# Sliding-window attention with SwiGLU on one core: V kept twice in DRAM in lines of 32-token rows, and projected by residue classes

## The chip, the core and the metric

The kernel runs on one core of a Trainium2 chip. The time is device microseconds of one execution. TensorE (PE) multiplies matrices into PSUM, VectorE (DVE), ScalarE (ACT) and GpSimd (POOL) work on SBUF and PSUM, and SyncE (SP) issues nearly all DMA transfers, which 16 DMA engines carry out. Each engine runs its instructions in order and waits on semaphores.

## What is computed

One transformer block with modulated layer norms, S = 2048 tokens, D = 512, 32 heads of 16, F = 1792. Each query sees W = 8 keys at distances 0, 2, ..., 14 before it.

```python
sa, ca, ga, sb, cb, gb = split(silu(c) @ w_mod, 6)
h = layernorm(x) * (1 + ca) + sa
q, k, v = heads(h @ wqkv)
idx = pos[:, None] - 2 * arange(8)[None, :]        # masked where idx < 0
attn = softmax(where(mask, einsum('hsd,hswd->hsw', q, k[idx]) / 4, -1e9))
x = x + ga * (einsum('hsw,hswd->hsd', attn, v[idx]) @ wo)
h = layernorm(x) * (1 + cb) + sb
x = x + gb * ((silu(h @ w1) * (h @ w3)) @ w2)
```

## The kernel before, in words

The 2048 tokens are 16 tiles T of 128. `LN1` (L270) groups the tiles for the first layer norm and the projections of q, k and v: two, two, four, four, four tiles. `BLOCKS` (L266) groups them for the softmax, `FFN` (L265) for the second layer norm and the FFN. The body of `_build` records operations by `p.op` and `p.dma` in a natural order, numbered from 0. The order in which they are issued on each engine is the list `ORDER` (L980) of these numbers, and the buffer of each tile is in `SLOTS` (L1028). Both lists are the output of a planner that worked with the costs that stand in the calls; for a DMA, `packet_ns` (L70) gives the time of one run, and loads marked `again` count 126 ns a run (L128). `synchronize` (L165) derives the semaphore waits from the operations' reads and writes; transfers of one `group` share one semaphore.

Layer norm writes normalized tiles, which are transposed by TensorE (L636) or by DMA (L617, issued at L124), and modulated by ScalarE (L621, L644) into `vh.at`, a buffer of 128 features by 4 feature blocks by up to 512 tokens. `proj_qk` (L675, matmuls L691) makes q and k with tokens along the free dimension. `proj_v` (L705) makes V of one tile with the tokens on the partitions: the weights of the matmul at L711 are 128 consecutive token columns of `vh.at`, the moving operand is the V part of `wqkv`. ScalarE evicts it (L721) with the heads innermost, and one DMA (L725) writes the tile as 128 rows of 1 KB to the scratch tensor `v_dram` in DRAM, which begins with 16 zero rows (L444).

The logits of a tile come from one multiplication on VectorE (L742, q against eight shifted views of k) and a sum over each head by TensorE (L752). After the softmax the attention weights are transposed by TensorE (L807) and copied to `val` (L811). `values` (L815) then does the weighted sum. Partition (s, w), with s = 0..15 and w = 0..7, gets copies of V's rows: group g = 2q + y of eight holds token 32q + 2s + y − 2w of the tile. Four DMAs, one for each q, load them (L820), each as 128 runs of 2 KB, two neighbouring tokens. So each row of V is read eight times. The load of tile T waits for the stores of T and T − 1, or of T and the zero rows. VectorE multiplies by the weights (L827), TensorE sums over the window (L855), ScalarE evicts (L861), a DMA transposes (L862), TensorE multiplies by `wo` (L867), and VectorE adds to x (L871).

The FFN (L883 up and gate, L889 silu, L892 product, L921 and L909 down) of the first tiles starts while the attention of later tiles still runs. `vshpool` has two buffers, and a third one, `vsh_x`, once the QKV weights are no longer read. Lines that matter for the change: L128, L340, L444, L705 to L726, L802 to L808, L815 to L822, L855 and L943 to L944, and the two lists.

Of the kernel before, what the change touches and what calls it, by code (L numbers as in the profile page):

```python
# [10 lines left out]
P = 128  # L11
S = 2048
D = 512
H = 32
DH = 16
W = 8
DIL = 2
F = 1792
NT = S // P
KT = D // P  # L20
NF = F // P
PAD = 16
EPS = 1e-5
# [50 lines left out]
class Program:  # L74
# [41 lines left out]
    def dma(self, out, in_, key, packets, r=(), w=(), part=(), after=(), eng="sp", cost=450, group=None, transpose=False,  # L116
# [11 lines left out]
        ns = 600 if transpose else each * (126 if again else packet_ns(size))  # L128
# [144 lines left out]
def _build(p, A_x, A_wqkv, A_wo, B_w1, B_w3, B_w2, c, w_mod, out):  # L273
# [66 lines left out]
    v_dram = nc.dram_tensor("v_scratch_dram", (PAD + S, D), bf)  # L340
# [103 lines left out]
    p.dma(v_dram[0:PAD, :], zrow[:], ("load", 11), (16, 1024), r=[vzrow] + wm_hold, w=[vvpad], store=True)  # L444
# [260 lines left out]
    def proj_v(T, tt, vh):  # L705
# [3 lines left out]
        def mm(e, ts):  # L709
            for t in ts:  # L710
                ins = e.matmul(bank(vp), vh.at[:, t, tt * P:(tt + 1) * P], wqkv[:, t, 2 * D:3 * D], start=(t == ORDER[0]),  # L711
                               stop=(t == ORDER[-1]))
            return ins
# [10 lines left out]
        vd = Val("vd")  # L724
        p.dma(v_dram[PAD + T * P:PAD + (T + 1) * P, :], lambda: vt.at[:], k, (128, 1024), r=[vt], w=[vd], cost=400, store=True)  # L725
        vv_dram[T] = vd  # L726
# [62 lines left out]
    def softmax(Ts, vl, ve, vx_):  # L789
# [12 lines left out]
        def turn(e):  # L802
            b = bank(vt).bitcast(bf)
            for i in range(n):
                at = b[:, i * 256:(i + 1) * 256].rearrange("p (q y h) -> p q y h", q=4, y=2)
                for y in range(2):
                    ins = e.transpose(at[:, :, y, :], bass.AP(ve.at[0], i * W * 32 + y * 16 * W, [[2 * W * 32, P], [1, P]]), ident[:])  # L807
            return ins  # L808
# [6 lines left out]
    def values(T, i, val):  # L815
# [3 lines left out]
        for q in range(4):  # L819
            p.dma(lambda q=q: vv.at[:, 2 * q:2 * q + 2, :],  # L820
                  bass.AP(v_dram, (PAD + T * P + 32 * q) * D, [[2 * D, 16], [-DIL * D, W], [1, 2 * D]]), ("vl", T), (128, 2048),
                  r=[vv_dram[T]] + ([vv_dram[T - 1]] if T else [vvpad]), part=[vv], group=loads, cost=640, again=True)  # L822
# [27 lines left out]
        else:  # L850
            def acc2(e):
                c0 = vo.at * 512
                for y in range(2):
                    for q in range(4):
                        ins = e.matmul(PALL[32 * q:32 * q + 32, c0:c0 + 512], ind2[:, y, :], vv.at[:, 2 * q + y, :], start=(y == 0),  # L855
# [82 lines left out]
    for gi, Ts in enumerate(LN1):  # L938
# [4 lines left out]
        for i, T in enumerate(Ts):  # L943
            proj_v(T, i, vh)  # L944
# [35 lines left out]
ORDER = [  # L980
# [96 lines left out]
```

## Time and profile before

| | |
|---|---|
| three runs | 238.4, 239.76, 240.06 us; median 239.76 |
| profiled execution: span from first to last instruction | 237.7 us |
| its time beside the span | not given apart; the runs' median is 2.06 us above the span, the fastest run 0.7 us |
| granted TensorE clock | 1.00 |
| packets of all DMA queues | 46317, 38.85 MB |
| HBM read and written | 29.62 MB and 4.21 MB |

How to read the profile: "busy" is the time in which an engine executes; PEld is TensorE's loading of weights, which overlaps its matmuls. L12 is line 12 of the kernel. In a timeline a row has the start, the length, the engine, the line and operation, what is written and read, how many of them, and in brackets the idle time before it with what ended it. "SPq" is the issuing of transfers on SyncE's queue, not the transfers themselves. Some records of matmuls are missing, so a row may count three where four ran. A matmul's record includes about 0.16 us in which the next one already streams.

### The profile page before, as it was taken

What the parts mean: (1) busy time and instruction counts of PE and PEld (TensorE: products, weight loads), DVE (VectorE), ACT (ScalarE), POOL (GpSimd) and SP (SyncE); (2) the same over time, 40 slices, a digit from 0 to 9 for tenths busy, and PEclk for the clock granted to TensorE, in tenths of its full rate; (3) what the DMA queues carried; (4) which work ended last, traced back from release to release, by engine and by line L of the source; (5) the groups of instructions that cost most, each with busy time, mean ns of one, the idle gap of its engine ahead of it and who ended that gap; (6) DMA issues with size and microseconds to landing.
All of it is one profiled execution on the core that took longest, in us unless ns stands there. A gap on an engine that the chain in (4) does not pass through costs nothing.

```text
span 237.7 us, 4535 instructions
## 1 busy us (share of the span) xinstructions
PE 229.7 (97%) x1781; PEld 136.2 (57%) x1806; DVE 179.4 (75%) x279; ACT 138.5 (58%) x267; POOL 29.2 (12%) x66
## 2 busy tenths in 40 slices
PE   7999999999999998999999999999999999999995
PEld 4776454445588674664444444444475457485774
DVE  5699999999999989999999999682654403434433
ACT  2289577999978744985865594837473405040300
POOL 4434100013002000240002520012010000000000
PEclk9999999999999999999999999999999999999999
DMA  6999999999999999897981693642203000000202
GB/s 216 372 337 322 158 237 299 208 269 283 353 200 270 243 249 199 173 260 177 247 234 47 182 234 72 154 132 46 67 19 91 3 0 0 6 19 0 70 0 88
DMA packets 46317, 38.85 MB, mean 163 GB/s; under 512 B 21704, under 2 KB 37080, under 8 KB 46296
## 3 DMA queue, kind: packets, MB, share of 16 engines
q1 hardware_dynamic: 46288, 38.56, 66.9%
q8 instruction: 14, 0.23, 0.4%
q14 instruction: 7, 0.06, 0.1%
q10 hardware_dynamic: 8, 0.00, 0.0%
HBM read 29.62 MB, written 4.21 MB: 142 GB/s over the span
## 4 chain that ended last, share of the span: by engine, by line
PE 74%; DMA 8%; DVE 8%; SPq 4%; ACT 3%; issue 2%; ACTq 0%; DVEq 0%
PE pall L883 38%; PE pall L921 18%; DMA sb_x<-in_A_x_dram 5%; PE pall L867 5%; SPq L124 4%; PE pall L691 4%; DMA sb_vsh<-v_scratch_dram 3%; PE pall L909 3%; PE pall L855 2%; PE pall L752 2%; PE pall L711 2%; DVE sb_vsh L827 2%; DVE sb_pq L742 2%; DVE sb_hh L892 1%; ACT sb_h L621 1%
## 5 line engine op out<-in xcount | busy, mean ns | idle before, releaser
L883 PE MATMUL pall<-sb_h,sb_w 128*128 128x256 bf16 (+1 forms) x664 | 101.9, 307 | 1.8 <-DVE sb_hh L892 0.9
L883 PEld LDWEIGHTS pall<-sb_h,sb_w 128*128 128x128 bf16 x672 | 64.8, 98 | 37.2 <-issue 2.8
L889 ACT ACTIVATE sb_sg<-pall 128x256 bf16<-128x256 f32 (+1 forms) x84 | 35.6, 453 | 54.1 <-PE pall L883 53.0
L892 DVE TENSOR_TENSOR sb_hh<-sb_sg,pall 128x256 bf16<-128x256 bf16 (+1 forms) x84 | 39.9, 505 | 34.8 <-PE pall L883 32.7
L921 PE MATMUL pall<-sb_w,sb_hh 128*128 128x512 bf16 x190 | 44.0, 379 | 0.3
L742 DVE TENSOR_TENSOR sb_pq<-sb_q,sb_kT 128x4096 bf16<-128x4096 bf16 x16 | 36.3, 2282 | 0.0
L921 PEld LDWEIGHTS pall<-sb_w,sb_hh 128*128 128x128 bf16 x196 | 19.0, 98 | 21.6 <-DVE sb_hh L892 0.4
L691 PE MATMUL pall<-sb_h,sb_wqkv 128*128 128x512 bf16 (+1 forms) x154 | 30.2, 335 | 0.5 <-issue 0.2
L827 DVE TENSOR_TENSOR sb_vsh<-sb_vsh,sb_al 128x4096 bf16<-128x4096 bf16 x12 | 27.3, 2287 | 2.1 <-DMA sb_vsh<-v_scratch_dram 2.1
L621 ACT ACTIVATE sb_h<-sb_h,sb_modc 128x512 bf16<-128x512 bf16 (+1 forms) x24 | 16.5, 743 | 10.1 <-DMA sb_h<-sb_xn 10.1
L691 PEld LDWEIGHTS pall<-sb_h,sb_wqkv 128*128 128x128 bf16 x160 | 14.7, 98 | 11.8 <-ACT sb_ac L861 0.4
L931 DVE TENSOR_TENSOR sb_o<-pall,sb_x 128x512 bf16<-128x512 f32 (+1 forms) x18 | 11.1, 625 | 10.5 <-PE pall L921 6.8
L711 PE MATMUL pall<-sb_wqkv,sb_h 128*128 128x512 bf16 x62 | 15.5, 379 | 0.2
L867 PE MATMUL pall<-sb_wo,sb_ot 128*128 128x512 bf16 x61 | 15.3, 379 | 0.3 <-issue 0.2
L586 POOL TENSOR_SCALAR sb_nm<-sb_sx 128x2 f32<-128x2 f32 x8 | 1.7, 218 | 105.2 <-DVE sb_x L871 105.1
L644 ACT ACTIVATE sb_h<-pall,sb_modc 128x256 bf16<-128x256 bf16 (+1 forms) x18 | 9.9, 612 | 7.5 <-DVE sb_modc L509 6.5
L861 ACT ACTIVATE sb_ac<-pall 128x512 bf16<-128x512 f32 x16 | 9.5, 595 | 7.2 <-PE pall L855 7.1
L601 ACT ACTIVATE sb_xn<-sb_x,sb_nb,sb_rs 128x512 bf16<-128x512 bf16 x16 | 12.4, 806 | 0.7 <-POOL sb_nb L599 0.6
L871 DVE SCALAR_TENSOR_TENSOR sb_x<-pall,sb_x 128x512 bf16<-128x512 f32 x16 | 10.9, 686 | 1.5 <-PE pall L867 1.3
L590 ACT ACTIVATE sb_xn<-sb_x,sb_nm 128x512 bf16<-128x512 bf16 x16 | 11.4, 714 | 0.7 <-POOL sb_nm L586 0.7
L721 ACT ACTIVATE sb_v<-pall 128x512 bf16<-128x512 f32 x16 | 9.5, 600 | 2.8 <-PE pall L711 2.8
L555 DVE BATCH_NORM_STATS2 sb_st<-sb_x 128x6 f32<-128x512 bf16 x16 | 10.6, 680 | 0.8 <-DMA sb_x<-in_A_x_dram 0.7
(87 smaller groups left out, 208.3 us busy)
## 6 DMA issues: line engine op xcount, KB each, us to landing
sb_vsh<-v_scratch_dram SPq DMA_DIRECT2D x48, 256.0 KB, 5.5
sb_vshx<-v_scratch_dram SPq DMA_DIRECT2D x16, 256.0 KB, 4.6
sb_w<-in_B_w_dram SPq DMA_DIRECT2D x6, 512.0 KB, 7.9
sb_w<-in_B_w_dram SPq DMA_DIRECT2D x6, 384.0 KB, 5.4
v_scratch_dram<-sb_v SPq DMA_DIRECT2D x16, 128.0 KB, 6.4
out_dram<-sb_o SPq DMA_DIRECT2D x14, 128.0 KB, 1.8
sb_wqkv<-in_A_wqkv_dram SPq DMA_DIRECT2D x6, 256.0 KB, 6.3
sb_x<-in_A_x_dram SPq DMA_DIRECT2D x4, 256.0 KB, 6.4
```

What stands on the lines that cost most here:

```text
L590: p.op("act", lambda e, vn=vn, T=T: e.activation(vn.at[:], x_sb[:, T, :], ACT.Square, bias=nm[:, T, :], accum_out=var[:, T, :]), c_act(512 ...
L601: p.op("act", lambda e, vn=vn, T=T: e.activation(vn.at[:], x_sb[:, T, :], ACT.Identity, bias=nb[:, T, :], scale=rs[:, NT + T, :]), c_act(5 ...
L621: return e.activation(vh.at[:, ft, 0:n * P], vh.at[:, ft, 0:n * P], ACT.Identity, bias=modc[:, 8 * which + ft:8 * which + ft + 1], scale=m ...
L691: ins = e.matmul(bank(vp)[:, j * n:(j + 1) * n], wqkv[:, t, col:col + P], vh.at[:, t, 0:n], start=(t == ORDER[0] and j == 0), stop=(t == O ...
L711: ins = e.matmul(bank(vp), vh.at[:, t, tt * P:(tt + 1) * P], wqkv[:, t, 2 * D:3 * D], start=(t == ORDER[0]), stop=(t == ORDER[-1]))
L742: return e.tensor_tensor(vp.at[:], in0, in1, ALU.mult)
L827: return e.tensor_tensor(v_w, v_w, a_w, ALU.mult)
L867: ins = e.matmul(bank(vy), vt.at[:, ft, :], wo[:, ft, :], start=(ft == 0), stop=(ft == KT - 1))
L883: ins = e.matmul(bank(vp)[:, 0:n], wt[:, t, fi * P:(fi + 1) * P], vh.at[:, t, 0:n], start=(t == 0), stop=(t == KT - 1))
L889: p.op("act", lambda e: e.activation(vt.at[:, 0:n], bank(vgp)[:, 0:n], ACT.Silu), c_act(n), k, r=[vgp], w=[vt], table="silu")
L892: p.op("dve", lambda e: e.tensor_tensor(vh_.at[:, 0:n], vt.at[:, 0:n], bank(vup)[:, 0:n], ALU.mult), c_dve(n), k, r=[vt, vup], w=[vh_])
L921: ins = e.matmul(bank(vz), vhh[fi].at[:, tt * P:(tt + 1) * P], w2[:, fi, :], start=(fi == 0), stop=(fi == NF - 1))
```

## The change

The scratch tensor becomes 64 lines of `VL` = 66 · 512 + 256 elements. Line 32 + r, for r from −32 to 31, holds token 32j + r at position j, one row of 512 elements each. So every token stands in two lines: token 32j + b in line 32 + b at position j, and in line b at position j + 1. A tile's copies for one y are then 16 by 8 runs of four rows (tokens 32 apart), 4 KB, from line 32 + y + 2s − 2w at position 4T, and two DMAs of 512 KB load a tile. The groups in the buffer are now g = 4y + q.

A V tile must hold tokens of which each partition's row goes to the right line. `proj_v` therefore takes, for a group of n tiles, every n-th token column beginning with b: n = 2 for tiles 0 to 3 and n = 4 for the others. Two DMAs of 128 runs of 1 KB store each result, one a copy. A value `vd` is common to a group, so the load of a tile waits for all stores of its group, and of the group before where tile T − 1 lies in that one. The planner's cost of a run loaded `again` is 160 ns instead of 126, for runs twice as long. `ORDER` and `SLOTS` are new lists (1102 operations instead of 1118).

```diff
+VL = 66 * D + 256
...
-        ns = 600 if transpose else each * (126 if again else packet_ns(size))
+        ns = 600 if transpose else each * (160 if again else packet_ns(size))
...
-    v_dram = nc.dram_tensor("v_scratch_dram", (PAD + S, D), bf)
+    v_dram = nc.dram_tensor("v_scratch_dram", (64, VL), bf)
...
-    p.dma(v_dram[0:PAD, :], zrow[:], ("load", 11), (16, 1024), r=[vzrow] + wm_hold, w=[vvpad], store=True)
+    p.dma(bass.AP(v_dram, 16 * VL, [[VL, PAD], [1, D]]), zrow[:], ("load", 11), (16, 1024), r=[vzrow] + wm_hold, w=[vvpad], store=True)
...
-    def proj_v(T, tt, vh):
+    def proj_v(Ts, b, vh):
+        n, T = len(Ts), Ts[b]
...
-                ins = e.matmul(bank(vp), vh.at[:, t, tt * P:(tt + 1) * P], wqkv[:, t, 2 * D:3 * D], start=(t == ORDER[0]),
+                ins = e.matmul(bank(vp), bass.AP(vh.at, 512 * t + b, [[KT * 512, P], [n, P]]), wqkv[:, t, 2 * D:3 * D], start=(t == ORDER[0]),
...
-        vd = Val("vd")
-        p.dma(v_dram[PAD + T * P:PAD + (T + 1) * P, :], lambda: vt.at[:], k, (128, 1024), r=[vt], w=[vd], cost=400, store=True)
-        vv_dram[T] = vd
+        for copy in range(2):
+            p.dma(bass.AP(v_dram, (32 * (1 - copy) + b) * VL + (4 * Ts[0] + copy) * D, [[D, 4 * n], [n * VL, 32 // n], [1, D]]), lambda: vt.at[:], k,
+                  (128, 1024), r=[vt], part=[vv_dram[T]], cost=400, store=True)
...
-                at = b[:, i * 256:(i + 1) * 256].rearrange("p (q y h) -> p q y h", q=4, y=2)
...
-                    ins = e.transpose(at[:, :, y, :], bass.AP(ve.at[0], i * W * 32 + y * 16 * W, [[2 * W * 32, P], [1, P]]), ident[:])
+                    ins = e.transpose(b[:, (2 * i + y) * P:(2 * i + y + 1) * P], bass.AP(ve.at[0], i * W * 32 + y * 16 * W, [[2 * W * 32, P], [1, P]]), ident[:])
...
-        for q in range(4):
-            p.dma(lambda q=q: vv.at[:, 2 * q:2 * q + 2, :],
-                  bass.AP(v_dram, (PAD + T * P + 32 * q) * D, [[2 * D, 16], [-DIL * D, W], [1, 2 * D]]), ("vl", T), (128, 2048),
+        for y in range(2):
+            p.dma(lambda y=y: vv.at[:, 4 * y:4 * y + 4, :],
+                  bass.AP(v_dram, (32 + y) * VL + 4 * T * D, [[2 * VL, 16], [-DIL * VL, W], [1, 4 * D]]), ("vl", T), (128, 4096),
...
-                        ins = e.matmul(PALL[32 * q:32 * q + 32, c0:c0 + 512], ind2[:, y, :], vv.at[:, 2 * q + y, :], start=(y == 0),
+                        ins = e.matmul(PALL[32 * q:32 * q + 32, c0:c0 + 512], ind2[:, y, :], vv.at[:, 4 * y + q, :], start=(y == 0),
...
-        for i, T in enumerate(Ts):
-            proj_v(T, i, vh)
+        vd = Val("vd")
+        for T in Ts:
+            vv_dram[T] = vd
+        for b in range(len(Ts)):
+            proj_v(Ts, b, vh)
...
```

On SP the new list runs, after the zero rows and decoded from its numbers: store of V tile 1, second store of 0, w1's third part, second store of 1, store of 0, transpose of tile 11, the second half of `wm_s[1]`, transpose of 10, tile 0's load for y = 1, transposes of 8 and 9, tile 0's load for y = 0. On TensorE the two reductions of the logits of tiles 2 and 3 now stand ahead of the first q or k matmuls of the group of tiles 8 to 11. SP has 152 entries instead of 168; TensorE 384, VectorE 263, ScalarE 241 as before.

131 rows, old and new, of tables (ORDER, SLOTS) are left out of this document.

## Prediction

> **What bounds the kernel now.** I read the page first, then the ten-microsecond windows of all engines, then who waited for whom, then the timelines of the engines at the places the waits named. The page and the windows (columns: length, busy us and instructions of PE, PEld, DVE, ACT, POOL, then clock, DMA share, GB/s):
>
> ```profile
> span 237.7 us, 4535 instructions
> PE 229.7 (97%) x1781; PEld 136.2 (57%) x1806; DVE 179.4 (75%) x279; ACT 138.5 (58%) x267; POOL 29.2 (12%) x66
> PE   7999999999999998999999999999999999999995
> q1 hardware_dynamic: 46288, 38.56, 66.9%
> ```
>
> ```profile
> 0.00:10.00 10.00, 8.07 (x79) 5.70 (x80) 6.84 (x26) 2.16 (x3) 4.42 (x20) 1.00 0.84 283
> 20.00:30.00 10.00, 9.83 (x97) 5.37 (x97) 10.00 (x18) 7.38 (x15) 2.49 (x5) 1.00 1.38 233
> 80.00:90.00 10.00, 9.13 (x99) 6.44 (x88) 8.82 (x9) 4.31 (x11) 0.00 (x0) 1.00 1.17 239
> 90.00:100.00 10.00, 9.59 (x70) 5.19 (x70) 9.86 (x19) 7.49 (x14) 0.62 (x4) 1.00 0.80 183
> ...
> 150.00:160.00 10.00, 9.95 (x50) 4.62 (x49) 7.19 (x10) 6.05 (x12) 0.70 (x2) 1.00 0.57 151
> ```
>
> TensorE is busy 97% of the span at full clock. The DMA engines are full as well (share 1.38 in 20 to 30 us, packets overlapping), and so is VectorE, but neither decides unless TensorE runs dry. TensorE's idle time is 237.7 − 229.7 = 8.0 us. Its timeline and the end of the chain that ended last show where:
>
> ```profile
> 1.24 1.68 PE L518 MATMUL pall<-sb_ones 128*128 128x256 bf16 x7 [1.24 <-DVE sb_ones L375]
> 63.94 4.09 PE L883 MATMUL pall<-sb_h,sb_w 128*128 128x256 bf16 x36 [0.23 <-DVE sb_attn L797]
> 89.82 1.05 PE L883 MATMUL pall<-sb_h,sb_w 128*128 128x256 bf16 x8 [0.87 <-DVE sb_hh L892]
> 93.19 0.61 PE L855 MATMUL pall<-sb_vsh,sb_ind 128*32 128x512 bf16 x8 [0.36 <-DVE sb_vsh L827]
> ```
>
> ```profile
> 96.51 1.51 PE pall L921 x7
> ...
> 235.06 0.42 DVE sb_o L931
> ```
>
> 1.2 us lie before the first matmul and 237.7 − 235.1 = 2.6 us after the last. That leaves 8.0 − 1.2 − 2.6 = 4.2 us in the middle, all that any schedule of the same matmuls can win. Three gaps of it are shown, 0.23, 0.87 and 0.36 us. (The chain's other row gives what a matmul of 512 columns takes in a stream: 1.51 / 7 = 0.216 us.) VectorE's timeline and the waits say why:
>
> ```profile
> 60.31 2.29 DVE L827 TENSOR_TENSOR sb_vsh<-sb_vsh,sb_al 128x4096 bf16<-128x4096 bf16 x1 [0.26 <-DMA sb_vsh<-v_scratch_dram]
> 87.14 2.29 DVE L827 TENSOR_TENSOR sb_vsh<-sb_vsh,sb_al 128x4096 bf16<-128x4096 bf16 x1 [1.04 <-DMA sb_vsh<-v_scratch_dram]
> 90.75 2.29 DVE L827 TENSOR_TENSOR sb_vsh<-sb_vsh,sb_al 128x4096 bf16<-128x4096 bf16 x1
> ...
> 158.73 2.29 DVE L827 TENSOR_TENSOR sb_vsh<-sb_vsh,sb_al 128x4096 bf16<-128x4096 bf16 x1 [0.85 <-DMA sb_vsh<-v_scratch_dram]
> ```
>
> ```profile
> DVE sb_vsh L827 <- DMA sb_vsh<-v_scratch_dram: 2.1, 3, 1.0
> ```
>
> At 87 us VectorE waited 1.04 us for a tile's copies of V. Its multiplications for the FFN, queued behind, came late, and TensorE waited 0.87 us for one and 0.36 us for the next weighted V. The 0.23 us at 63.9 follow a DMA wait of 0.26 us in the same way. So V's loads cost the path 0.87 + 0.36 + 0.23 = 1.46 us, although VectorE waits 2.1 us for them in all: the third wait, 0.85 us at 158 us, lies where VectorE is busy 7.19 us of 10 and TensorE 9.95.
>
> **The change part by part.** *Loads.* A tile's four transfers of 256 KB become two of 512 KB; the bytes stay, the runs grow from 2 to 4 KB, 32 issues go. *Stores.* Each V tile goes out twice: 16 more transfers of 128 KB. The rows:
>
> ```profile
> sb_vsh<-v_scratch_dram SPq DMA_DIRECT2D x48, 256.0 KB, 5.5
> sb_vshx<-v_scratch_dram SPq DMA_DIRECT2D x16, 256.0 KB, 4.6
> v_scratch_dram<-sb_v SPq DMA_DIRECT2D x16, 128.0 KB, 6.4
> v_scratch_dram<-sb_zrow SPq DMA_DIRECT2D x1, 16.0 KB, 9.5
> ```
>
> The loads are 64 × 256 KB = 16.8 MB of the 38.6 MB. In 90 to 100 us, where they make up most of the traffic, the queues ran at 183 GB/s for a share of 0.80, so 229 GB/s at full share; in the first 10 us, where inputs are read once, 283 / 0.84 = 337. At 229 the loads fill all engines for 73 us; if long runs bring 337, for 50. The doubled stores add 2.1 MB, 6.2 us at 337. Estimated from these rows, the DMA engines are 17 us less loaded if runs are what slows the loads, and 6 to 9 us more if not. None of it is on the path by itself; on the path are the 1.46 us above. Bounds: −1.46, and +1.2 if the loads are no faster and 9.2 us of stores, 0.6 us a tile, come on top at the two places that reach TensorE. I take −1.46: half of the 73 − 50 = 23 us, spread over 16 tiles, is 0.7 us a tile, against waits of 1.04 and 0.26.
>
> The Trainium skill ("DMA: Bandwidth & Descriptors", Specifications) says that a transfer needs runs of 512 B or more for line rate. By that rule 2 KB and 4 KB runs move alike and the term would be 0 instead of −1.46. The two rates above speak partly for it, as the fast window also reads runs of 1 and 2 KB: what is slow may be the eightfold re-reading, which stays. It is a rival below.
>
> *V projected by residue classes.* Same 64 weight loads and 64 matmuls, but a weight column is now taken at steps of two tokens (tiles 0 to 3) or four (tiles 4 to 15):
>
> ```profile
> L711 PE MATMUL pall<-sb_wqkv,sb_h 128*128 128x512 bf16 x62 | 15.5, 379 | 0.2
> L711 PEld LDWEIGHTS pall<-sb_wqkv,sb_h 128*128 128x128 bf16 x64 | 6.1, 98 | 6.6 <-ACT sb_v L721 0.4 <-ACT sb_q L700 0.2
> ```
>
> A load of 98 ns lies under a matmul that streams for 216. A faster load would not shorten a stream, so no gain. If four-step reads took four times as long, 392 ns, each of 48 matmuls would lose 392 − 216 = 176 ns, 8.4 us. Nearest is the same instruction with its 98 ns: I take 0. The Trainium skill ("SBUF — State Buffer", the DMA port swizzle) has 16-byte lines that give full rate from two hits a line on; a step of four 2-byte values is two hits, so it too gives 0; no run here shows it.
>
> The other edits move no work: the transposed attention weights land in PSUM contiguously instead of in two halves, V's multiplication and the sum over the window count the eight groups in another order, and the zero rows go to 16 lines instead of one block. Cost 0, on the same instructions of the same sizes. SP issues 16 transfers fewer in all; at the 0.46 to 0.69 us of the rows below that is 7 to 11 us of a queue that is on the path only where it makes a tile late.
>
> *The waits added.* A tile's loads now wait for every store of its projection group, both copies, where before one tile's and its predecessor's sufficed. Tiles 0 and 1 need four landings instead of two, and the new list puts that load in a dangerous place. SP, ScalarE and TensorE before:
>
> ```profile
> 14.73 2.59 SPq L124 DMA_DIRECT2D v_scratch_dram<-sb_zrow  x1
> 17.36 0.91 SPq L124 DMA_DIRECT2D v_scratch_dram<-sb_v  x2
> 18.31 0.46 SPq L124 DMA_DIRECT2D sb_wm_s<-in_w_mod_dram  x1
> 21.03 5.66 SPq L124 DMA_TRANSPOSE sb_h<-sb_xn  x4
> 26.80 5.55 SPq L124 DMA_DIRECT2D sb_vsh<-v_scratch_dram  x8
> ```
>
> ```profile
> 30.61 2.96 ACT L621 ACTIVATE sb_h<-sb_h,sb_modc 128x512 bf16<-128x512 bf16 x4
> ```
>
> ```profile
> 33.33 1.89 PE L691 MATMUL pall<-sb_h,sb_wqkv 128*128 128x512 bf16 x7
> ...
> 40.55 0.63 PE L752 MATMUL pall<-sb_pq,sb_E 128*32 128x256 bf16 x16
> 41.00 0.61 PE L855 MATMUL pall<-sb_vsh,sb_ind 128*32 128x512 bf16 x8
> ```
>
> Before, the four transposes of tiles 8 to 11 stood ahead of all V loads. In the new list SP has, after the zero rows: store, store, 384 KB of w1, store, store, transpose of tile 11, weights, transpose of 10, tile 0's first load, transposes of 8 and 9. At 0.46 us an issue the fourth store goes out at 17.36 + 4 × 0.46 = 19.2 us and, by the median of 6.4, lands at 25.6. SP reaches the load at 21.03 + 2 × 1.42 + 0.46 = 24.3 (5.66 / 4 = 1.42 a transpose) and waits 1.3 us. Behind it stand the two transposes: 25.6 + 0.69 + 2.83 = 29.1. Before, the last one's issue ended at 26.7 and ScalarE began on the group at 30.6, at most 3.9 us later; so it begins at 33.0 and ends at 36.0. TensorE's first matmul of that group stood, behind four of another, at 33.33 + 4 × 0.216 = 34.2; the new list puts two reductions of 0.45 us (40.55 to 41.00) ahead: 35.1. TensorE, which runs in order, stands still for 36.0 − 35.1 = **0.9 us**. Bounds: 0, and 4.0 if the store takes the 9.5 us of the zero rows' store.
>
> Later groups have cover: the last store of tiles 12 to 15 is close ahead of tile 12's load, but SP then waits anyhow for a buffer that VectorE holds:
>
> ```profile
> 120.56 7.60 SPq L124 DMA_DIRECT2D sb_vsh<-v_scratch_dram  x2
> ```
>
> Without that cover it would be 6.4 us less two transposes of 1.42 in between, 3.6 us on SP, and the transposes for the FFN behind it.
>
> *The new order.* Counted from the lists, TensorE has 384 entries before and after, VectorE 263, ScalarE 241; only SP changes, 168 to 152. Bounds: −2.7 (4.2 less the 1.46 already counted), and +8.0 if all fourteen windows from 20 to 160 us were as idle as 80 to 90 (14 × 0.87 = 12.2, less 4.2). The list fills the same engines with the same work, so I take 0, nearest to the present idle.
>
> **Sum.** 237.7 − 1.46 + 0.9 = 237.1 us of span. The three runs' median is 239.76, 2.06 above the profiled span, and I keep that distance: **239.2 us**. A measurement of this kernel, whose three runs spread over 0.7%, tells about 1%, that is 2.4 us, from no change.
>
> **Rivals.** *Middle filled:* the load in time, no wait on V, and half of the other 2.7 us gone with the freer DMA: −1.46 − 1.35 = −2.8, **237.0**. For it: the full DMA share in 20 to 30 and 80 to 90 us; against it: only 2.1 us of DMA waits stand in VectorE's rows.
>
> *First load holds SP (slower):* the same place as my 0.9, with the store landing in 9.5 us: load at 28.7, transposes out at 32.2, ScalarE done at 39.1, TensorE 4.0 us dry; −1.46 + 4.0 = +2.5, **242.3**. It makes the kernel slower from 7.0 us of landing on, 0.6 above the median: the stall is then the 1.46 us that the loads win. For it: the share of 1.38 just there, with stores doubled and w1 ahead; against it: the median of 6.4.
>
> *Runs don't matter:* the eightfold re-reading makes the loads slow, not the runs; the 1.46 us stay and the 0.9 comes on top: **240.7**. The change then does not do what it says. For it: 337 GB/s were reached with runs of 1 and 2 KB; against it: those windows differ in more than the re-reading.
>
> *Strided weights:* four-fold loads, +8.4 − 0.6 = **247.5**. No row speaks for it.
>
> **How the numbers follow.** My forecast 0.40, middle filled 0.25, first load holds SP 0.20, runs don't matter 0.12, strided weights 0.03. Faster by over 1% is below 237.4: 0.23 of the middle filled and 0.04 of mine, 0.27. Slower by over 1% is above 242.2: 0.16 of the held SP, 0.03 of the weights, 0.03 of mine and 0.02 of runs that don't matter, 0.24. The rest, 0.49, is within 1%. The range, 236.4 to 242.8, takes in the cases on both sides and ends between half and all of the middle gone (237.0 and 235.6) below; my own case alone is 238.3 (no stall) to 240.7 (no gain).
>
> **What would show it.** Right: sb_vsh loads at two a tile, landing per byte sooner than 5.5 us for 256 KB; no DMA wait ahead of L827 before 100 us; L711 weight loads still at 98 ns; 229 to 231 us of PE busy. The added wait shows as a gap in SP's timeline ahead of the first V load and in TensorE's ahead of group 3's projection near 35 us. Wrong: weight loads above 200 ns, a DMA share that did not fall after 60 us, or more than 5 us of TensorE idle in the middle.

## The result and the profile after

The changed kernel takes 251.77 us (median of four runs, 250.49 to 252.8) against 239.91 for the kernel before beside it: slower, ratio 1.051 [1.046, 1.057]. The prediction was 239.2 us with a range to 242.8. All ratios here leave out executions more than 1.5% above the fastest of their kernel, which takes three of six from e12 and a few elsewhere.

The page of the changed kernel, first the span, the engines, TensorE's forty slices and the granted clock, then the queue that carries nearly all transfers (packets, MB, share of 16 engines):

```profile
span 248.7 us, 4534 instructions
PE 232.0 (93%) x1781; PEld 136.6 (55%) x1806; DVE 178.2 (72%) x279; ACT 138.1 (56%) x267; POOL 25.0 (10%) x66
PE   7999979749997989899999999999999999999995
PEclk9999999979999999999999999999999999999999
q1 hardware_dynamic: 43920, 40.66, 67.6%
```

The span grew by 11.0 us. TensorE's idle time went from 8.0 to 16.7 us, of which 16.7 − 1.2 − 2.6 = 12.9 lie in the middle; the prediction had named more than 5 as a sign of being wrong. Its busy time grew by 2.3 at the same work. The queue's share rose from 66.9% to 67.6%, of a longer span: nothing was freed, though 2368 packets are gone. Ten-microsecond windows of the changed kernel (columns as before):

```profile
30.00:40.00 10.00, 8.44 (x98) 4.63 (x99) 9.48 (x18) 6.18 (x11) 3.25 (x3) 1.00 1.08 273
40.00:50.00 10.00, 7.97 (x50) 3.20 (x49) 7.82 (x6) 8.05 (x16) 0.00 (x0) 1.00 1.00 196
50.00:60.00 10.00, 6.93 (x51) 3.07 (x53) 5.35 (x7) 4.77 (x10) 0.27 (x2) 0.83 1.05 271
70.00:80.00 10.00, 8.41 (x69) 5.78 (x69) 8.57 (x14) 8.09 (x16) 0.22 (x1) 1.00 1.15 202
90.00:100.00 10.00, 8.85 (x69) 6.43 (x69) 7.72 (x12) 7.24 (x14) 0.00 (x0) 1.00 1.09 259
```

Between 30 and 60 us TensorE is idle for 6.7 us, against 0.3 in the kernel before. TensorE's timeline names the gaps:

```profile
36.84 0.81 PE L692 MATMUL pall<-sb_h,sb_wqkv 128*128 128x512 bf16 x3 [1.51 <-ACT sb_h L622]
45.36 0.62 PE L856 MATMUL pall<-sb_vsh,sb_ind 128*32 128x512 bf16 x8 [1.41 <-DVE sb_vsh L828]
52.91 3.15 PE L868 MATMUL pall<-sb_wo,sb_ot 128*128 128x512 bf16 x8 [3.37 <-DMA sb_ot<-sb_ac]
77.88 1.04 PE L868 MATMUL pall<-sb_wo,sb_ot 128*128 128x512 bf16 x4 [1.53 <-DMA sb_ot<-sb_ac]
91.63 2.79 PE L884 MATMUL pall<-sb_h,sb_w 128*128 128x256 bf16 x24 [1.10 <-ACT sb_v L723]
101.11 1.04 PE L868 MATMUL pall<-sb_wo,sb_ot 128*128 128x512 bf16 x4 [0.82 <-DMA sb_ot<-sb_ac]
```

Those six make 9.7 us: group 3's h is late, then the weighted V, then three times the transposed attention output, once an eviction of V. VectorE's wait ahead of the second gap is a load of V, 2.18 us late:

```profile
43.02 2.29 DVE L828 TENSOR_TENSOR sb_vsh<-sb_vsh,sb_al 128x4096 bf16<-128x4096 bf16 x1 [2.18 <-DMA sb_vsh<-v_scratch_dram]
```

What the transfers take from issue to landing, and V's weight loads (by line):

```profile
sb_vsh<-v_scratch_dram SPq DMA_DIRECT2D x26, 512.0 KB, 6.8
v_scratch_dram<-sb_v SPq DMA_DIRECT2D x32, 128.0 KB, 6.1
```

```profile
L713 PEld LDWEIGHTS pall<-sb_wqkv,sb_h 128*128 128x128 bf16 x64 | 6.4, 111 | 5.3 <-issue 0.4 <-ACT sb_kT L702 0.3
```

The strided weights are harmless. The loads, per transfer, land 1.3 us later than the 256 KB ones did (5.5). Per byte that is sooner, as the prediction's sign of being right had it, but the five windows above show 196 to 273 GB/s and not the 337 that it counted on.

### The profile page after: what moved, and what is told of

Read it like the earlier page. It is cut to its first block, busy times and chain, and to the rows that moved or that the text cites. A ratio compares the mean times of both kernels' runs of the same rounds, so it can differ in the third digit from the quotient of the medians.

```text
span 248.7 us, 4534 instructions
## 1 busy us (share of the span) xinstructions
PE 232.0 (93%) x1781; PEld 136.6 (55%) x1806; DVE 178.2 (72%) x279; ACT 138.1 (56%) x267; POOL 25.0 (10%) x66
## 3 DMA queue, kind: packets, MB, share of 16 engines
q1 hardware_dynamic: 43920, 40.66, 67.6%
## 4 chain that ended last, share of the span: by engine, by line
PE 60%; DMA 18%; DVE 9%; ACT 6%; SPq 5%; issue 2%; ACTq 0%; DVEq 0%
PE pall L884 33%; PE pall L922 13%; DMA v_scratch_dram<-sb_v 7%; DMA sb_ot<-sb_ac 6%; PE pall L868 6%; DMA sb_x<-in_A_x_dram 5%; SPq L125 5%; DVE sb_pq L744 4%; PE pall L910 2%; PE pall L856 1%; PE pall L692 1%; PE pall L754 1%; ACT sb_v L723 1%; DVE sb_st L556 1%; DVE sb_vsh L828 1%
## 5 line engine op out<-in xcount | busy, mean ns | idle before, releaser
L890 ACT ACTIVATE sb_sg<-pall 128x256 bf16<-128x256 f32 (+1 forms) x84 | 36.1, 454 | 58.5 <-PE pall L884 52.5
L922 PE MATMUL pall<-sb_w,sb_hh 128*128 128x512 bf16 x188 | 42.9, 379 | 0.5 <-issue 0.2
L828 DVE TENSOR_TENSOR sb_vsh<-sb_vsh,sb_al 128x4096 bf16<-128x4096 bf16 x13 | 29.7, 2288 | 6.3 <-ACT sb_al L812 3.8
L868 PE MATMUL pall<-sb_wo,sb_ot 128*128 128x512 bf16 x60 | 16.5, 404 | 6.0 <-DMA sb_ot<-sb_ac 5.7
L587 POOL TENSOR_SCALAR sb_nm<-sb_sx 128x2 f32<-128x2 f32 x8 | 2.4, 297 | 125.5 <-DVE sb_x L872 125.5
L868 PEld LDWEIGHTS pall<-sb_wo,sb_ot 128*128 128x128 bf16 x64 | 6.1, 101 | 13.6 <-issue 4.9
```

Source lines behind the costliest of these rows:

```text
L828: return e.tensor_tensor(v_w, v_w, a_w, ALU.mult)
L868: ins = e.matmul(bank(vy), vt.at[:, ft, :], wo[:, ft, :], start=(ft == 0), stop=(ft == KT - 1))
L890: p.op("act", lambda e: e.activation(vt.at[:, 0:n], bank(vgp)[:, 0:n], ACT.Silu), c_act(n), k, r=[vgp], w=[vt], table="silu")
L922: ins = e.matmul(bank(vz), vhh[fi].at[:, tt * P:(tt + 1) * P], w2[:, fi, :], start=(fi == 0), stop=(fi == NF - 1))
```

## The experiments

Medians in microseconds, ratios to runs of the kernel before on the same chip; that kernel's medians there were 239.0 to 239.5. "Old order" is the kernel before's `ORDER` with `SLOTS`, its entries renumbered.

**Layout and order apart.** e1 is the changed code under the old order, a tile's two loads in the places of the old list's first two of four, the second store right behind the first; e2 the kernel before under the new list.

> The changed kernel (new lines, two stores a tile, two loads a tile, residue classes) in the order and buffers of the kernel before: of the four loads of a tile the first two places are kept, the second store stands right behind the first. Theory O (the new order is at fault: it was planned with loads that are 37% faster than they are): 239 to 242 us. Theory L (the layout is at fault: two stores a tile fill SP and hold the three V buffers until both have landed, so that ScalarE waits): 246 us or more, with waits of ScalarE's V eviction on the stores of 4 us or more.

> The kernel before (one store a tile, four loads of 2 KB runs, one block) in the order and buffers of the changed one: each new load's place is taken by two old ones, a tile's store stands where its first copy stood. Theory O: 246 us or more. Theory L: 239 to 242 us.

e1: 253.4, 1.059 [1.053, 1.066], in the range of theory L, but ScalarE waited only 2.6 us for the stores and not 4 or more. e2: 245.09, 1.023 [1.019, 1.027], between the two forecasts. Each costs by itself, and they do not add up: the new list costs the old layout 2.3%, and on the new one it is if anything better than the old list (1.051 against 1.059, with intervals that overlap). e2's page and its largest gaps:

```profile
PE 232.9 (96%) x1806; PEld 135.8 (56%) x1806; DVE 178.2 (73%) x279; ACT 138.2 (57%) x267; POOL 25.1 (10%) x66
```

```profile
37.17 1.04 PE L691 MATMUL pall<-sb_h,sb_wqkv 128*128 128x512 bf16 x4 [1.86 <-ACT sb_h L621]
45.27 0.61 PE L855 MATMUL pall<-sb_vsh,sb_ind 128*32 128x512 bf16 x8 [0.78 <-DVE sb_vsh L827]
50.79 1.89 PE L867 MATMUL pall<-sb_wo,sb_ot 128*128 128x512 bf16 x8 [1.34 <-ACT sb_h L621]
```

With four more between 67 and 120 us (0.56, 0.78, 0.31, 0.77) they make 6.4 us; the span is 6.0 us longer than before's. This profile also has all 1806 matmul records, the one before only 1781. Beside these seven gaps, the two ends and one gap of 0.44 us at 3.35 us, e2's TensorE is idle for under 0.1 us. The kernel before has the same early gap, 0.43 us, and the 1.46 us of the prediction's three. The other 2.3 of its 4.2 us in the middle are spots of 0.16 us and less, nearly all of them records that are missing: there was about 1.9 us to win, not 4.2.

**V's buffers, and the second copy under the new list.** e3 gives V six SBUF buffers; e4 leaves out the second stores and reads lines of the first copy only.

```diff
-    vb = [sb([P, D], bf, f"v{i}") for i in range(3)]
+    vb = [sb([P, D], bf, f"v{i}") for i in range(6)]
```

```diff
-        for copy in range(2):
+        for copy in range(1):
...
-bass.AP(v_dram, (32 + y) * VL + 4 * T * D, [[2 * VL, 16], [-DIL * VL, W], [1, 4 * D]])
+bass.AP(v_dram, (46 + y) * VL + 4 * T * D, [[VL, 16], [-DIL * VL, W], [1, 4 * D]])
```

> The changed kernel, same order, with six SBUF buffers for V tiles instead of three, given out in turn. Theory L in its form that the buffers hold ScalarE up: the 7.3 us of V evictions waiting on stores go, and the time falls by 4 to 7 us, to 245 to 248. Theory O, or that SP's queue is at fault: a fall of under 2 us.

> The changed kernel, same order, without the second store of each tile. The loads read the upper 32 lines alone (one line a step instead of two), so V's rows are the wrong tokens; sizes and run lengths stay. Theory L: 240 to 244 us. Theory O: 248 us or more, since the order and the slow loads stay.

e3: 251.18, 1.050 [1.045, 1.056]; ScalarE no longer waits for stores, and the time is the same, so the idea that the doubled stores hurt by holding V's buffers fell. e4: 247.61, 1.036 [1.030, 1.042], between its two forecasts; the second copy is 1.5% of the 5.1, about 3.6 us.

**The load forms by themselves.** p1, run once, computes nothing. It loads 16.8 MB five times over SyncE: the old form, the new form, 2 KB runs of x with each row read once, 4 KB runs of x once, 4 KB runs of the new lines once. "Once" means once in the loads of two tiles (four for the lines); over the whole stretch each row comes again, but megabytes later.

> Nothing of the block is computed: x is brought in, written to DRAM as the old block and as the new lines, and then the transfers of 16 tiles (16.8 MB) run alone, form after form with a wait between them: the old loads (2 KB runs, each row read eight times), the new loads (4 KB runs, read eight times), 2 KB runs of x read once a transfer, 4 KB runs of x read once, 4 KB runs of the new lines read once. Theory of longer runs: the new loads take under 0.75 of the old ones' time, about 50 us against 73. Rival, re-reading sets the rate: old and new loads take the same time within 10%, and the forms read once are at least 1.3 times as fast, at either run length. Rival, the line pitch slows them: the last form is as slow as the new loads.

Windows inside the five stretches, with the DMA share and GB/s as the last two columns:

```profile
32.00:96.00 64.00, 0.00 (x0) 1.00 1.04 253
100.00:166.00 66.00, 0.00 (x0) 1.00 1.02 244
172.00:214.00 42.00, 0.00 (x0) 1.00 1.05 378
216.00:256.00 40.00, 0.00 (x0) 1.00 0.98 388
262.00:302.00 40.00, 0.00 (x0) 1.00 1.01 398
```

Rows read eight times come at 253 GB/s in 2 KB runs and 244 in 4 KB runs; rows read once at 378, 388 and 398. Re-reading in close succession takes a third off the rate; the old forms also step backwards from key to key, and no run separates that. The run changes the rate by under 4% between 2 and 4 KB, and lines far apart do not lower it. (`VL` is 68096 bytes, so the lines are 66.5 KB apart; the texts on record say 67.5.)

**Parts alone, old order.** e5: the kernel before with a second store that nothing reads. e6: the changed code with one copy, loads in the places of e1. e7: the kernel before with residue classes and the wait for a group's stores.

```diff
+        p.dma(v2_dram[PAD + T * P:PAD + (T + 1) * P, :], lambda: vt.at[:], k, (128, 1024), r=[vt], cost=400, store=True)
```

```diff
-        p.dma(v_dram[PAD + T * P:PAD + (T + 1) * P, :], lambda: vt.at[:], k, (128, 1024), r=[vt], w=[vd], cost=400, store=True)
+        p.dma(bass.AP(v_dram, (PAD + Ts[0] * P + b) * D, [[n * D, P], [1, D]]), lambda: vt.at[:], k, (128, 1024), r=[vt], part=[vv_dram[T]],
+              cost=400, store=True)
```

> The kernel before in its own order, with each V tile stored a second time, right behind the first, to a tensor that nobody reads. Theory D (the second store costs DMA and SP time in the stage where both are full, and holds the V buffers longer, and this is most of the loss): 246 us or more. Rival (the stores hide, the slow new loads or the group waits cost): 239 to 242 us.

> The changed kernel in the order of the kernel before, without the second store; the loads are two of 512 KB with 4 KB runs from the upper 32 lines alone, so V's rows are the wrong tokens. Theory D: 240 to 244 us. Rival (loads of 512 KB or the group waits cost): 246 us or more.

> The kernel before in its own order, block and loads, with V projected by residue classes and one store a tile to every second or fourth row; a load waits for all stores of its group. Theory D: 239 to 242 us, weight loads of the V projection still 98 ns. Rival (strided weights or the group waits cost): 244 us or more, with weight loads above 200 ns or VectorE's waits on V's loads grown.

e5: 245.14, 1.022 [1.015, 1.029]. e6: 245.12, 1.020 [1.012, 1.029]. Both lie between their two forecasts. e7: 239.46, 1.002 [0.999, 1.005]. So under the old order residue classes and group waits are free, and the store and the new loads cost 5 to 6 us each, which is most of e1's 14. SyncE's timeline of e5, and one row of the kernel before, show the store's price:

```profile
22.61 6.57 SPq L124 DMA_TRANSPOSE sb_h<-sb_xn  x4
29.30 5.45 SPq L124 DMA_DIRECT2D sb_vsh<-v_scratch_dram  x8
...
40.59 5.33 SPq L124 DMA_TRANSPOSE sb_h<-sb_xn  x3
...
47.56 1.27 SPq L124 DMA_TRANSPOSE sb_ot<-sb_ac  x1
```

```profile
43.27 1.27 SPq L124 DMA_TRANSPOSE sb_ot<-sb_ac  x1
```

In the kernel before the loads begin at 26.80 and so 2.5 us sooner; by the first transpose of the attention output (43.27 there) SyncE is 4.3 us late. Seven second stores stand ahead of it, with 3.1 us of issues.

**Place in the queue.** e8 is e6 with a tile's loads in the places of the old list's second and fourth. e9 is e5 with the second store issued by ScalarE. e10 is the whole new layout with both. e11 is the changed kernel with one stretch of SyncE's list rearranged:

```diff
-tr 10, load 0, tr 8, tr 9, load 0, store 2, store 3, store 2, load 1, store 5, store 5, load 1
+tr 10, tr 8, tr 9, load 0, load 0, load 1, load 1, store 2, store 3, store 2, store 5, store 5
```

(The numbers are tiles; "tr" is the transpose of h.)

> The kernel of e6 (the new transfers of 512 KB, one copy only, so that part of V's rows are wrong tokens, the old order), with one difference: e6 put a tile's two transfers where the old list had its first and second of four, this one where the old list had its second and fourth. So no transfer is issued before all of the bytes that the old list had issued there. Theory 'position': e6 lost its 6 us because half of each tile's bytes were moved ahead in SP's and the DMA engines' queues, ahead of other work (at 116 us 1 MB of copies in front of the transposes of sb_ot, whose matmul then stood 2.11 us; at the start tile 0's second half behind tile 1's). Then most of it comes back: 239 to 241.5 us. Rival 'form': a transfer of 512 KB with 4 KB runs is itself worse among other traffic than two of 256 KB with 2 KB runs: 244 to 246 us as in e6. In the load probe both forms moved bytes alike (253 and 244 GB/s).

> The kernel of e5 (before, with every V tile stored a second time to a tensor that nothing reads), with the second store issued by ScalarE, one instruction behind the eviction of the tile, instead of by SP. The bytes are those of e5. Theory 'position': e5's 6 us come from 16 issues more in SP's queue, 0.43 to 0.5 us each, ahead of transposes and loads of V (the first loads were issued at 29.3 us instead of 26.8): then 239 to 241 us, with up to 1 us for the issues on ScalarE. Rival 'bytes': 2.1 MB more in full DMA engines delay all landings: 243 to 246 us as in e5.

> The whole new layout (lines, two copies, two transfers of 512 KB a tile, residue classes), with the old order, a tile's transfers where the old list had its second and fourth, and the second store issued by ScalarE behind the eviction. Nothing of the computation is left out. Theory 'position': what e1 lost (14 us) was lost in SP's queue: then 239 to 243 us, near before but not below it, because re-reading moves at the same rate. Rival 'bytes and form': the doubled stores and the large transfers cost what they cost wherever they are issued: 250 us or more, as e1 had 253.4.

> The changed kernel with one stretch of SP's list in another order: behind the transpose of tile 10 come the transposes of tiles 8 and 9, then the two loads of tile 0 and the two of tile 1 in a row, and then the five V stores that stood between them. Theory 'order': the stall of 1.5 us ahead of group 3's first matmul at 36.8 us goes (nothing waits on a store's landing ahead of the transposes), tile 1's copies are issued at about 32 instead of 35.1 us and land 2 to 3 us sooner, and the stalls of 1.4 and 3.4 us at 45 and 53 us shrink with them: 247 to 249 us against 251.8. Rival 'elsewhere': the stalls at 45 and 53 us are set by the transposes of the attention output or by the stores that now come later: 250.5 us or more.

e8: 245.47, 1.025 [1.021, 1.029]: "position" fell for the loads, the form itself costs. e9: 242.5, 1.014 [1.011, 1.017]: between the two forecasts. Off SyncE the store costs 1.4% instead of 2.2%; the intervals overlap a little, so it is likely, not sure, that about a third of its price was SyncE's queue. The rest, 3.3 us, lies with the bytes or with ScalarE's issues. e10: 251.08, 1.047 [1.041, 1.053]: a miss for "position". e11: 252.41, 1.056 [1.051, 1.060]: a miss for "order". Its profile shows why it gained nothing: group 3 came almost in time, but the stores now stood behind the loads, ScalarE waited for V's buffers, and TensorE for ScalarE:

```profile
36.10 0.81 PE L692 MATMUL pall<-sb_h,sb_wqkv 128*128 128x512 bf16 x3 [0.39 <-ACT sb_h L622]
44.82 1.89 PE L692 MATMUL pall<-sb_h,sb_wqkv 128*128 128x512 bf16 x4 [4.22 <-ACT sb_v L723]
```

```profile
ACT sb_v L723 <- DMA v_scratch_dram<-sb_v: 12.8, 6, 4.7
```

**Order and faster loads.** e12 is e11 with six V buffers, e13 is e2 with the same rearrangement and six buffers. e15 loads a tile by four transfers of 256 KB with 4 KB runs, 64 each. e16 is the kernel before with the copies read from x, each row once in two tiles; its loads still wait for the V stores, although its text below says that they do not.

```diff
-bass.AP(v_dram, (PAD + T * P + 32 * q) * D, [[2 * D, 16], [-DIL * D, W], [1, 2 * D]])
+bass.AP(x2d.tensor, x2d.offset + ((T % 2) * 1024 + q * 256) * D, [[2 * D, P], [1, 2 * D]])
```

```diff
-            p.dma(lambda y=y: vv.at[:, 4 * y:4 * y + 4, :],
-                  bass.AP(v_dram, (46 + y) * VL + 4 * T * D, [[VL, 16], [-DIL * VL, W], [1, 4 * D]]), ("vl", T), (128, 4096),
+            p.dma(lambda y=q // 2, h=64 * (q % 2): vv.at[h:h + 64, 4 * y:4 * y + 4, :],
+                  bass.AP(v_dram, (46 + q // 2 + 8 * (q % 2)) * VL + 4 * T * D, [[VL, 8], [-DIL * VL, W], [1, 4 * D]]), ("vl", T), (64, 4096),
```

> The kernel of e11 with six SBUF buffers for V instead of three. In e11 the five stores behind the loads in a row left late, and ScalarE waited 12.8 us for them, TensorE 4.2 us at 44.8 us. Theory 'order': with the buffers that wait goes, and what the earlier loads bring shows: the stalls at 36 us (0.4), 45 and 53 us together fall from 6.3 us in the changed kernel to 3 or less, 247.5 to 249.5 us. Rival 'landing': the stalls come from what the DMA engines can land by then, whatever is issued first: 251 us or more.

> The kernel of e2 (the old layout and loads under the new order) with the first loads of tiles 0 and 1 in a row behind the transposes of tiles 8 and 9, and six V buffers. e2 lost 5.9 us; its TensorE stalls were 1.86 us for group 3 at 37 us, 0.78 at 45, 1.34 at 51, 0.56 at 67, 0.78 at 74, 0.31 at 95 and 0.77 at 120. Theory 'order': the first two go and some of the third: 241.5 to 243.5 us against 245.1. Rival 'rest of the list': what is gained at the start is lost at the next late transpose: 244.5 us or more.

> The kernel of e6 and e8 (lines, one copy only, so that part of V's rows are wrong tokens, the old order), with each tile's copies loaded by four transfers of 256 KB, as before, each with 64 runs of 4 KB, in exactly the old list's places. Theory 'runs': 4 KB runs out of lines 67.5 KB apart move at 230 GB/s in the stretch from 75 to 92 us where e7's 2 KB runs move at 249 (read from the packets), and that stretch ends with the loads: 243 to 246 us, as e6 and e8. Rival 'size': large transfers hold up the rest, four small ones are as good as before: 239 to 241 us.

> The kernel before, with the copies of V read from rows of x, each row once, instead of V's rows eight times each; bytes, runs (2 KB), transfers, places and waits for buffers are the same, but the loads wait for no V store (V's values are wrong). In the load probe this form moved 378 GB/s against 253. Theory 'edge': the loads end last in the stretch from 60 to 92 us, so TensorE's stalls of 0.87, 0.36 and 0.23 us go, and the gain that the prediction expected of long runs appears: 237 to 238.5 us. Rival 'hidden': other work takes their place and nothing changes: 238.7 to 239.7 us.

e12: 1.050 [1.044, 1.056], the ratio of the changed kernel, though the median of all six runs is 253.4. e13: 245.25, 1.023 [1.019, 1.027], that of e2. "Order" in the sense of the first loads' place fell in both layouts; which places of the new list lose the time was not narrowed down further. e15: 286.04, 1.196 [1.192, 1.200], of no use for the question, since its transfers ran at half rate (below). e16: 238.39, 0.998 [0.995, 1.001]; its profiled span is 236.2 against 237.7. Windows of e16, and of the kernel before at the same place:

```profile
72.00:76.00 4.00, 4.00 (x37) 3.29 (x36) 3.92 (x10) 3.99 (x12) 0.61 (x3) 1.00 1.07 406
86.00:90.00 4.00, 4.00 (x42) 3.12 (x39) 4.00 (x6) 1.93 (x6) 0.00 (x0) 1.00 0.43 115
```

```profile
86.00:90.00 4.00, 3.13 (x30) 2.58 (x28) 2.96 (x4) 1.42 (x4) 0.00 (x0) 1.00 1.33 224
```

With loads at 406 GB/s the 0.87 us stall of 86 to 90 us is away (TensorE 4.00 of 4 instead of 3.13), and the span is 1.5 us shorter. That is the gain that the prediction expected of long runs, seen in one profiled execution of each, and it is too small for the runs to tell it from none.

**The run alone.** e17 is e6 with four transfers of 256 KB, 128 runs of 2 KB each, in the old list's places; e18 is e10 with the same loads.

```diff
-            p.dma(lambda y=y: vv.at[:, 4 * y:4 * y + 4, :],
-                  bass.AP(v_dram, (46 + y) * VL + 4 * T * D, [[VL, 16], [-DIL * VL, W], [1, 4 * D]]), ("vl", T), (128, 4096),
+            p.dma(lambda y=y, c=c: vv.at[:, 4 * y + 2 * c:4 * y + 2 * c + 2, :],
+                  bass.AP(v_dram, (46 + y) * VL + (4 * T + 2 * c) * D, [[VL, 16], [-DIL * VL, W], [1, 2 * D]]), ("vl", T), (128, 2048),
```

> The kernel of e6 (V in lines, one copy only, so that part of V's rows are wrong tokens, residue classes, the old order), with each tile's copies loaded by four transfers of 256 KB in exactly the old list's places, each with 128 runs of 2 KB (half of a 4 KB run). Theory 'run': two transfers with 4 KB runs are what costs 6 us, in 230 GB/s against 249 and in landing as a whole: 239 to 241 us. Rival 'lines': storing and reading in lines 67.5 KB apart costs, whatever the run: 244 to 246 us, as e6 and e8.

> The kernel of e10 (the whole new layout, both copies, the second store issued by ScalarE, the old order; nothing of the computation is left out), with the loads of e17: four transfers of 256 KB with 2 KB runs. Theory 'run': e10's 251.1 us fall to about the 242.5 us of e9, which has the same stores without the lines: 241.5 to 244 us. Rival 'lines': 248 us or more.

e17: 239.38, 1.002 [0.999, 1.005], as theory "run" had it. e18: 248.0, 1.038 [1.033, 1.043], a miss for it. With one copy and the old order, lines, residue classes and stores into lines are free; two transfers with 4 KB runs in place of four with 2 KB cost the 6 us. VectorE's waits for copies of V and two windows, of e8 and then of e17:

```profile
DVE sb_vsh L828 <- DMA sb_vsh<-v_scratch_dram: 6.9, 5, 2.9
```

```profile
76.00:82.00 6.00, 5.95 (x54) 4.76 (x54) 5.97 (x11) 5.38 (x14) 1.31 (x4) 1.00 1.04 240
82.00:86.00 4.00, 4.00 (x47) 2.36 (x46) 3.95 (x4) 2.65 (x6) 0.00 (x0) 1.00 1.03 223
```

```profile
DVE sb_vsh L829 <- DMA sb_vsh<-v_scratch_dram: 0.7, 1, 0.7
```

```profile
76.00:82.00 6.00, 5.95 (x62) 3.71 (x62) 6.00 (x9) 4.86 (x11) 1.09 (x3) 1.00 1.07 246
82.00:86.00 4.00, 4.00 (x51) 2.89 (x49) 3.82 (x5) 1.58 (x5) 0.00 (x0) 1.00 1.07 251
```

Between 76 and 86 us nearly everything in the queues is copies of V. They move at 223 to 240 GB/s in the new form and at 246 to 251 in the old one, and VectorE waits 6.9 us for them in the whole execution instead of 0.7. Estimated from these four rows the lower rate makes only 0.6 us of the stretch; how the 6 us come together was not traced. Whether the run or the size of a transfer makes the difference is open: e15 was to separate them and did not. e18's median is 3.1 us below e10's (the intervals overlap a little), so in the whole layout about half of the loads' price came back.

Of the rest of e18's 8.9 us, beyond the 3.3 of e9, a part can be seen in its trace. At 63.94 us TensorE has stood 2.62 us for the second layer norm, and 0.51 us more follow. Two small steps on GpSimd ahead of it, of 2 values a partition, take 0.19 and 0.70 us where VectorE runs no multiplication of 4096 columns; here they took 2.26 and 2.70. TensorE, GpSimd and VectorE in e18, and the first of these steps in the kernel before:

```profile
63.94 0.29 PE L637 MATMUL pall<-sb_ident,sb_xn 128*128 128x128 bf16 x2 [2.62 <-ACT sb_xn L602]
56.30 2.26 POOL L597 TENSOR_SCALAR sb_rs<-sb_var 128x2 f32<-128x2 f32 x1 [2.26 <-ACT sb_xn L591]
56.23 2.28 DVE L744 TENSOR_TENSOR sb_pq<-sb_q,sb_kT 128x4096 bf16<-128x4096 bf16 x1
```

```profile
52.75 0.19 POOL L596 TENSOR_SCALAR sb_rs<-sb_var 128x2 f32<-128x2 f32 x1 [1.64 <-ACT sb_xn L590]
```

The step began inside VectorE's multiplication and ended with it (58.56 and 58.51 us). In the kernel before it had ended before the multiplication at 53.31 began. In e9 the same two gaps make 0.9 us. What remains beside these is not settled.

## Why the prediction was wrong

**Loads, taken at −1.46: this step failed first.** It needed runs of 4 KB to bring the 337 GB/s of the first windows. The rival *runs don't matter* had the missing gain right: re-reading sets the rate (253 against 378 GB/s in p1), and the change keeps it. The rule of the Trainium skill ("DMA: Bandwidth & Descriptors", Specifications) that runs from 512 B on move alike agrees with p1's 378 and 388 GB/s for 2 and 4 KB; by it the term was 0. Both are still too good by 5 to 6 us, the price that e8 and e17 show for the new form under the old order. That a few per cent less rate became so much because the copies had no slack is argued, not shown. I had counted the places where VectorE's wait for a load reached TensorE. In the landings in the trace of the kernel before the weighted sums of tiles 2, 4, 5, 6, 7 and 14 begin 0.02 to 0.1 us after their last load has landed: at six tiles the load ended last, whether or not the row showed a wait. A delay at the first can pass to the next, since each frees a buffer late for a later load. The bound of +1.2 priced two places.

**Doubled stores, taken at no cost on the path.** They cost 2.2% alone, 5 to 6 us (e5). "SP issues 16 transfers fewer in all" was true of the whole list and false of the part that mattered: up to 48 us the transposes of h, the loads of V and the transposes of the attention output all pass through SyncE, and there each second store pushes what follows back by 0.42 to 0.51 us (e5's issues of the second store). With the store on ScalarE's queue 3.3 us stay.

**The new order, taken at 0.** It costs 5.9 us with the old layout (e2), inside the bound of +8.0. The argument that the same engines do the same work says nothing of what waits for what; e2's seven gaps come where a transposed h, a load of V or a transposed attention output is late. The list's own cost for a copy, 160 ns a 4 KB run where two runs of 2 KB count 252, supposes that longer runs come faster; the runs show that they do not. That this made the list is argued, not shown.

**The wait added, +0.9.** The place was right and the size lay within the bounds of 0 and 4.0, but that was luck, for the cause was another. TensorE stood 1.51 us at 36.84, group 3's first matmul, but no store held SyncE. SyncE's waits from 18 to 36 us, and its timeline:

```profile
SPq L125 <- DVE sb_xn L577: 3.0, 1, 3.0
```

```profile
22.80 1.30 SPq L125 DMA_TRANSPOSE sb_h<-sb_xn  x1
24.16 1.70 SPq L125 DMA_DIRECT2D sb_wm_s<-in_w_mod_dram  x1
25.91 1.20 SPq L125 DMA_TRANSPOSE sb_h<-sb_xn  x1
27.30 0.63 SPq L125 DMA_DIRECT2D sb_vsh<-v_scratch_dram  x1
27.97 2.57 SPq L125 DMA_TRANSPOSE sb_h<-sb_xn  x2
```

It waited 3.0 us for the normalized tile 11, so it reached the load at 27.1 instead of the 24.3 of the prediction. By then the stores had landed, the last at 26.8 instead of 25.6. e7 agrees: under the old order waiting for a whole group's stores costs nothing. *First load holds SP* did not come about either.

**Right:** that the strided weight loads stay hidden, the edits priced at nothing, and the place of the first stall. The mean of 111 ns mixes two steps: in the trace of the changed kernel the 16 loads at steps of two tokens (tiles 0 to 3) took 98 ns as before, and the 48 at steps of four took 111 to 131, still under a stream of 216. By the line rule of the Trainium skill ("SBUF — State Buffer", the DMA port swizzle), which the prediction drew on, both steps have the full rate; the 111 to 131 ns of the step of four do not agree with it.

**The sum.** With their measured sizes under the old order the terms come to about +6 for loads and +6 for stores, near the 14 us of e1. Along the new list the ratios add up to the change itself: 2.3% for the list (e2), 1.3% more with the new loads (e4), 1.5% more with the second copy. There the order, taken at 0, is the largest of the three. *Middle filled* counted on the 4.2 us of idle time, of which more than half were missing records.

No run beat the kernel before by more than its uncertainty; e16's profile marks what is left: 1.5 us of span for loads that read each row once.

## What to carry to other kernels

Before pricing a faster transfer, ask what makes it slow: here rows fetched eight times over, which longer runs did not mend. Find slack from landings, not from waits: a consumer that starts within 0.1 us of a landing has none, even where the waits show nothing. An in-order issuing engine is priced by what stands ahead of the critical transfer at that moment, not by its total.

## What the runs showed of the hardware

- Reading rows eight times in close succession ran at 244 to 253 GB/s, reading each once in two or four tiles' loads at 378 to 398, with the same runs and nearly the same share of DMA time (0.98 to 1.05).
- Transfers of 64 runs, whose source pattern begins with a dimension of 8, ran at half rate. Windows of e15 where its copies are nearly alone in the queues:

```profile
91.00:94.00 3.00, 2.95 (x29) 2.52 (x28) 3.00 (x7) 2.39 (x7) 1.09 (x3) 1.00 0.51 125
97.00:100.00 3.00, 2.45 (x20) 1.18 (x21) 3.00 (x3) 1.88 (x4) 0.00 (x0) 1.00 0.50 120
```

  The share is 0.5, so half of the engines carry them; in the trace each of these transfers raises its semaphore nine times, where the others do it sixteen times. The Trainium skill ("DMA: Bandwidth & Descriptors", "Why a DMA increments its semaphore by 16 and not by 1") says that the number of engines must divide the slowest dimension of both patterns; 8 engines agree with that. The change itself has eight such transfers: for groups of two tiles its stores' pattern in DRAM begins with a dimension of 8, and the eight stores of tiles 0 to 3 show nine updates each, one soon after the issue and eight at the landing. e17 has four such stores and is as fast as the kernel before, so four of them cost nothing there.
- A GpSimd step of 128 by 2 values that begins while VectorE multiplies 128 by 4096 values (2.28 us) ends 0.05 to 0.06 us after that multiplication, or 0.56 us after it for the step that takes 0.70 us alone: so did all five such steps in the trace of the kernel before and all seven in that of e18.
- The granted clock fell to 0.83 in the window of the 3.37 us stall, and the eight matmuls at L868 behind it took 3.15 us, where the same eight of e2 took 1.89; that is 1.26 of the 2.3 us of added busy time. e1 stood 3.60 us at 131 us and kept a clock of 1.000, so not every such stall costs clock.
